# Converting double-precision weights on three engines: the split between VectorE and GpSimd, and two pieces of feed-forward held for the next block

## The chip, the cores and the metric

The kernel runs on one core of a Trainium2 chip. The core has five engines, each with an instruction queue of its own that it works through in order: TensorE (PE, with PEld for its weight loads), VectorE (DVE), ScalarE (ACT), GpSimd (POOL) and SyncE (SP), whose queue here only starts DMAs. Engines wait for each other through semaphores. The metric is the time of one execution in microseconds (us) on the device.

## The reference

Attention in which each query keeps only its 32 largest scores, and then a feed-forward layer with a hardswish gate. The attention's output is the input of the feed-forward layer.

```python
scores = scale * np.matmul(q, k.transpose(0, 1, 3, 2))      # (8, 8, 576, 64) each
kth = np.partition(scores, -32, axis=-1)[..., -32:-31]
scores = np.where(scores >= kth, scores, -1e9)
attn = softmax(scores)                                       # with 1e-9 in the denominator
x = (attn @ v) as (4608, 512)
h = x @ w_in                                                 # (512, 2048)
g = h * np.clip(h + 3.0, 0.0, 6.0) / 6.0
out = g @ w_out                                              # (2048, 512)
```

q, k and v are float32. [...]

## The kernel before

**Duos.** The work is cut into 80 duos. A duo is two pairs of heads and one tile of 128 queries; for the last 64 queries of a batch it is a rest duo, with one tile instead of two for each pair. For each duo TensorE makes the scores (`scores`, L225) into PSUM, and ScalarE copies them to SBUF (L271). VectorE then finds the 32 largest of each row: `top` (L276) takes four rounds of MAX8 (L283), and between them MATCH_REPLACE8 (L287) strikes out what was found. For each of the duo's two halves u (0 and 1) then follow: `shift` on GpSimd (L296, L299), `exp` on ScalarE (L306 and L311, with the sum into `den`, L316), `inverse` on VectorE (the reciprocal, L320), `weights` on GpSimd (L330 scales, L339 splits the words into halves for a transpose), `flip` (a DMA transpose from SP's queue), `join` (L351, which puts the halves together again, on ScalarE or GpSimd), and for both halves together `values` on TensorE (L371) and `place` (L381, a copy to xT on ScalarE).

**Steps.** The order of the work is written out by hand. The main loop takes each duo m through 8 steps i, and in each step VectorE gets one round of `top`. Step i of duo m is slot 8m + i of the whole order. The tables `usual`, `behind`, `early` and `soon` (L570 to L583) say how many steps after a duo's start each of the parts above is put into the queues. For duos 0 and 1 (`early`) the reciprocal comes one step after the exponentials; for the others it comes five steps after them.

**Feed-forward.** Every second duo completes 128 rows of x, and `queue` (L471) then adds a block of 16 pieces: eight of the first matmul (16 matmul records each, L398) and eight of the second (4 records each, L418). After every other one of the first eight, ScalarE reads h (L406, L408), and two pieces later a gate follows on GpSimd (L412, L413). At the end of each step `due` (L639) says how many pieces TensorE gets: one where any are left, a fraction more where 24 or 48 are left, half of it in rest duos. After the last duo the steps go on for three more duos without VectorE work, and then the pieces that are left follow one after another. The outputs of both matmuls, `values` and (in this kernel) the converted `y` share three PSUM buffers (`ps_w`).

**Conversion.** There are 32 chunks of 128 x 512 weights, 16 of w_in and 16 of w_out. `convert` (L96) is a generator, and `convert_step` (L522) advances three chunks by one stage each, once before and once after the first transposes and then once in every step until no chunk is left. A float64 is the words `lo` and `hi`, and they lie side by side, so each is read with a stride of two. For a chunk, in order:

- a DMA into a staging tile `st`;
- on ScalarE `y` = 2 + lo x 2^-51 (L109), into PSUM for the first 24 chunks and straight into the weight's place for the last 8, and the absolute value of `hi` read as a float, into the place of `lo` (L112); on GpSimd a clamp of that (L113);
- two steps later on VectorE a shift left by three bits (L118), and an operation with two inputs that takes the sign bit out of `hi` and puts it into `y` (L119);
- one step later on GpSimd the integer sum of both (L124), which is the float32 weight.

In a step, the sum of one chunk comes first, then VectorE's part of another, then ScalarE's part and the clamp of a third, then the next DMA. In the first four duos `shift` and `exp` stand ahead of the conversion within a step, and `inverse` and `weights` behind it.

**The start.** The first pair is transposed on its own: ScalarE copies its parts out of PSUM one after another (L195 to L197 and L187), and then the first scores in three copies (L271), so that VectorE can begin.

Of the kernel before, what the change touches and what calls it, by code (L numbers as in the profile page):

```python
# [8 lines left out]
AF = mybir.ActivationFunctionType  # L9
ALU = mybir.AluOpType  # L10
F32 = mybir.dt.float32
U32 = mybir.dt.uint32
I32 = mybir.dt.int32
# [11 lines left out]
HI_LEAST = 2.0**-15  # L25
HI_MOST = 122880.0 - 2.0**-7
# [3 lines left out]
def kernel(  # L30
# [9 lines left out]
    nc = tc.nc  # L40
    P = nc.NUM_PARTITIONS
# [3 lines left out]
    JP = J * P  # L45
    R = S - JP
    NHP = H // 2
    NFC = FF // P
    assert 2 * D == P and 2 * R == P and NHP * P == DM and B % 2 == 0
    assert JP == 512 and DM == 512 and TOP_K % 8 == 0  # L50
    scale = 1.0 / float(D) ** 0.5

    def pool(name, bufs, **kw):
        return ctx.enter_context(tc.tile_pool(name=name, bufs=bufs, **kw))
# [8 lines left out]
    gpool = pool("g", 8)  # L63
# [3 lines left out]
    ps_w = pool("ps_w", 3, space=PSUM)  # L67
# [20 lines left out]
    def big():  # L88

        return ps_big.tile([P, 5 * 512], F32, tag="big", name="big")  # L90
# [2 lines left out]

    WC = 512

    def convert(dst, src, early):  # L96

        st = kqpool.tile([P, 2 * WC], U32, tag="kq", name="st")
        nc.sync.dma_start(st[:], src)
        yield
        words = st[:].rearrange("p (n two) -> p n two", two=2)
        lo, hi = words[:, :, 0], words[:, :, 1]
        y = ps_w.tile([P, WC], F32, tag="w", name="y")[:] if early else dst

        nc.scalar.activation(y, lo, AF.Copy, bias=2.0, scale=2.0**-51)  # L109

        a = lo.bitcast(F32)
        nc.scalar.activation(a, hi.bitcast(F32), AF.Abs)  # L112
        nc.gpsimd.tensor_scalar(a, a, HI_MOST, HI_LEAST, ALU.min, ALU.max)  # L113
        yield

        nc.vector.tensor_scalar(lo, lo, 3, None, ALU.logical_shift_left)  # L118
        nc.vector.scalar_tensor_tensor(  # L119
            out=dst.bitcast(U32), in0=hi, scalar=0x80000000, in1=y.bitcast(U32),  # L120
            op0=ALU.bitwise_and, op1=ALU.bitwise_or,
        )
        yield
        nc.gpsimd.tensor_tensor(  # L124
            dst.bitcast(I32), lo.bitcast(I32), dst.bitcast(I32), ALU.add
        )

    def weight_chunks():
# [11 lines left out]
    class Pair:  # L140
# [31 lines left out]

        def transpose(self, first=False):

            kq = kqpool.tile([P, JP + S], F32, tag="kq", name="kq")
            self.kT, self.qT = kq[:, 0:JP], kq[:, JP : JP + S]
            c0 = 2 * JP

            def turn(ps, tiles):
                for i, j in enumerate(tiles):  # L180
                    rows = self.landed[:, j, :, :].rearrange("p h d -> p (h d)")
                    nc.tensor.transpose(ps[:, i * P : (i + 1) * P], rows, ident[:])  # L182

            def copy_left(ps):
                for hh in range(2):
                    d = slice(hh * D, (hh + 1) * D)
                    nc.scalar.copy(self.kr[d, hh, :], ps[d, 0:R])  # L187

            if first:

                ps = [ps_w.tile([P, 512], F32, tag="w", name="kqp") for _ in range(3)]
                turn(ps[0], range(J))
                turn(ps[1], [J, 2 * J])
                turn(ps[2], range(J + 1, 2 * J))
                nc.scalar.copy(self.kT, ps[0][:])  # L195
                nc.scalar.copy(kq[:, JP : JP + P], ps[1][:, 0:P])
                copy_left(ps[1][:, P:])  # L197
                self.later = [
                    (kq[:, JP + P : c0], ps[2][:, 0 : JP - P]),
                    (kq[:, c0 : c0 + R], ps[1][:, P + R : 2 * P]),  # L200
                ]
                return
            ps = big()
            turn(ps, range(2 * J + 1))
            nc.scalar.copy(kq[:, 0:c0], ps[:, 0:c0])
            nc.scalar.copy(kq[:, c0 : c0 + R], ps[:, c0 + R : c0 + 2 * R])
            copy_left(ps[:, c0:])

    class Duo:
# [15 lines left out]
        def scores(self, us=(0, 1)):  # L225

            if us[0] == 0:
                self.sc = scpool.tile([P, 2, 2 * (S + R)], F32, tag="sc", name="sc")
                self.den = mpool.tile([P, 2, 2], F32, tag="den", name="den")
            sc, nu = self.sc[:, us[0] : us[-1] + 1, :], len(us)  # L230
            ps = big()
            heads = [slice(0, D), slice(D, P)]
            qs = slice(self.qt * P, min(self.qt * P + P, S))
            banks = ps[:, 0 : 4 * 512].rearrange("p (n s) -> p n s", s=512)
            left = ps[:, 4 * 512 :]
            if self.rest:


                quarters = [
                    (i, hh, d, heads[u ^ hh])  # L240
                    for i, u in enumerate(us)
                    for hh, d in enumerate(heads)
                ]
                for i, hh, d, to in quarters:
                    pr = self.pairs[us[i]]
                    nc.tensor.matmul(banks[to, i, :], pr.qT[d, qs], pr.kT[d, :])
                for i, hh, d, to in quarters:
                    pr = self.pairs[us[i]]
                    nc.tensor.matmul(banks[to, 2 + i, 0:R], pr.qT[d, qs], pr.kr[d, hh, :])
                nc.gpsimd.memset(sc[:, :, S : S + R], 0.0)  # L250
                nc.scalar.copy(sc[:, :, 0:JP], banks[:, 0:nu, :])
                nc.scalar.copy(sc[:, :, JP:S], banks[:, 2 : 2 + nu, 0:R])
                return
            for i, u in enumerate(us):
                pr = self.pairs[u]
                nc.tensor.matmul(  # L256
                    left[:, i * P : (i + 1) * P], pr.qT[:, qs], pr.kr[:].rearrange("p h r -> p (h r)")
                )
            for i, u in enumerate(us):
                pr = self.pairs[u]  # L260
                for hh, d in enumerate(heads):
                    nc.tensor.matmul(banks[:, 2 * i + hh, :], pr.qT[d, qs], pr.kT[d, :])  # L262
            copies = [
                (sc.rearrange("p u (h s) -> p (u h) s", h=2)[:, :, 0:JP], banks[:, 0 : 2 * nu, :]),
                (sc[:, :, JP : JP + P], left[:, 0 : nu * P].rearrange("p (u r) -> p u r", r=P)),
            ]
            if us == (0,):
                (to, src), rest = copies
                copies = [rest, (to[:, 0, :], src[:, 0, :]), (to[:, 1, :], src[:, 1, :])]
            for copy in copies:  # L270
                nc.scalar.copy(*copy)  # L271

        def row(self, u, t):
            return self.sc[:, u, t * S : (t + 1) * S]
# [171 lines left out]
    ND = len(duos)  # L446
# [4 lines left out]
    left = 0  # L451
# [60 lines left out]
    chunks = list(weight_chunks())  # L512
    landing, converting, adding = [], [], []

    def land(count=1):

        for _ in range(min(count, len(chunks))):
            c = convert(*chunks.pop(0), early=len(chunks) >= NFC // 2)
            next(c)
            landing.append(c)  # L520

# [26 lines left out]
    ps = big()  # L548
    for _ in range(2):
        nc.tensor.matmul(ps[:, 0:DM], w_out[:, 0, 0:P], w_out[:, 0, :])  # L550
    first[0].load(nc.scalar)
    first[1].load()
    land()
    first[2].load()
    land()
    first[0].transpose(first=True)
    duos[0].scores((0,))
    for copy in first[0].later:
# [17 lines left out]
    early = dict(  # L576
        shift0=3, exp0=3, inverse0=4, weights0=4, flip0=5, join0=8,
        shift1=7, exp1=7, inverse1=8, weights1=8, flip1=9, join1=12, values=12, place=13,
    )
# [27 lines left out]
    due = 0.0  # L607
    for m in range(ND + 3):
        u = duos[m] if m < ND else None
        for i in range(8):  # L610
            if u:
                u.top(i // 4, i % 4)
            if m < 4:
                parts(8 * m + i, False)
            convert_step()
            if m == 0 and i in (1, 2):
                first[i + 1].transpose()
            if i == (4 if m == 0 else 1) and m + 1 < ND:
                duos[m + 1].scores()
            if m < 4:  # L620
                parts(8 * m + i, True)
            else:
                parts(8 * m + i)
            if m == 0 and i in (1, 4):
                for p in duos[i // 4].pairs:
                    p.load_values()
            if i == 0:
                p = pair_at(m, 4)
                if p:
                    p.load()  # L630
            if i == 3 and u and u.pairs[0].b and 1 <= m % per_batch <= 2:
                for p in duos[m - 1].pairs:
                    p.load_values()
            if i == 5:
                p = pair_at(m, 5)
                if p:
                    p.transpose()

            due += ((left > 0) + (left >= 24) / 8 + (left >= 48) / 8) / (2 if u and u.rest else 1)  # L639
            piece(int(due))  # L640
            due -= int(due)
    while todo:
# [35 lines left out]
```

## Time and profile before

| | |
|---|---|
| median of 3 runs | 1565.45 us (1564.18 to 1566.11) |
| the profiled execution | 1565.89 us, span 1564.1 us |
| VectorE busy | 1465.7 us (94%) |
| TensorE busy | 1445.2 us (92%) |
| GpSimd busy | 1136.3 us (73%) |
| ScalarE busy | 1098.6 us (70%) |
| L118, L119 (VectorE) | 32 x 896 ns; 24 x 675 ns with `y` in PSUM, 8 x 1041 ns with `y` in SBUF |
| L113, L124 (GpSimd) | 32 x 710 ns; 32 x 1.33 to 1.36 us |
| L109, L112 (ScalarE) | 32 x 630 to 687 ns; 32 x 680 ns |

The span runs from the first to the last instruction of the profile; the execution's time has a little more around it. A group's line gives the line of the kernel, the engine, the operation, the tiles (out<-in), the shapes and the count, then the busy time and the mean duration of one, then the idle time of the engine just before these instructions and what ended it. Busy shares are means over a kernel whose stages differ: the conversion happens in the first 141 us only, and the last 64 us have no VectorE work in them.

### The profile page before, as it was taken

To read this page: it belongs to the slowest core of one execution; us is meant where nothing else is said; L and a number is where in the kernel's file an instruction comes from. 1 tells how busy PE (TensorE), PEld (TensorE's weight loads), DVE (VectorE), ACT (ScalarE), POOL (GpSimd) and SP (SyncE) were. 2 spreads that over 40 slices of the span, in tenths; PEclk is the share of its full clock that TensorE was granted. 3 is DMA by queue.
4 is the path that set the end of the run, shared out by engine and by line. 5 is a ranking of instruction groups with operands and counts; after the bars stand their busy time and mean duration, and the time that the engine had idled before them with its cause. 6 is when DMAs were issued, how large, how long until landed. Compare 5 with 4: busy or idle time off the path is not lost.

```text
span 1564.1 us, 28780 instructions
## 1 busy us (share of the span) xinstructions
PE 1445.2 (92%) x10276; PEld 1033.0 (66%) x10276; DVE 1465.7 (94%) x3106; ACT 1098.6 (70%) x1868; POOL 1136.3 (73%) x1264
## 2 busy tenths in 40 slices
PE   5257798899999999999999999999999999999899
PEld 3143665677767777767776777677777777666675
DVE  6999999999999998999999999999999999999910
ACT  6676777677777777777777777777777777777631
POOL 3769688677777788677777778777777778777761
PEclk7568899999999999999999999999999999999999
DMA  8552445344444445355344454554344555433420
GB/s 225 160 196 57 103 83 113 74 93 81 69 83 99 98 86 108 73 100 93 76 83 85 100 96 83 89 99 98 69 83 83 99 99 92 95 68 68 79 42 14
DMA packets 450319, 144.49 MB, mean 92 GB/s; under 512 B 433280, under 2 KB 441472, under 8 KB 450176
## 3 DMA queue, kind: packets, MB, share of 16 engines
q1 hardware_dynamic: 448976, 142.36, 44.9%
q8 instruction: 81, 1.33, 0.3%
q14 instruction: 62, 0.51, 0.1%
q10 hardware_dynamic: 1200, 0.30, 0.1%
HBM read 45.09 MB, written 9.44 MB: 35 GB/s over the span
## 4 chain that ended last, share of the span: by engine, by line
DVE 42%; PE 42%; POOL 7%; ACT 4%; issue 4%; DMA 2%; SPq 1%; POOLq 0%; DVEq 0%; ACTq 0%
DVE m L283 22%; DVE wk L287 19%; PE h L398 16%; PE acc L418 15%; PE pv L371 5%; PE big L262 3%; POOL e L339 2%; POOL sc L330 1%; POOL g L413 1%; PE big L182 1%; POOL eT L351 1%; DMA t<-e 1%; PE big L256 1%; ACT sc L311 1%; ACT eT L351 1%
## 5 line engine op out<-in xcount | busy, mean ns | idle before, releaser
L283 DVE MAX8 m<-wk 128x8 f32<-128x576 f32 x864 | 614.6, 750 | 2.2
L418 PE MATMUL acc<-w_out,g 128*128 128x512 f32 x1152 | 522.1, 604 | 10.5 <-POOL g L413 10.5
L398 PEld LDWEIGHTS h<-xT,w_in 128*128 128x128 f32 x4096 | 472.1, 193 | 39.4 <-issue 21.7
L398 PE MATMUL h<-xT,w_in 128*128 128x128 f32 x4096 | 485.2, 278 | 14.0 <-ACT xT L381 13.1
L287 DVE MATCH_REPLACE8 wk<-m,wk 128x576 f32<-128x576 f32 x576 | 424.7, 746 | 0.0
L418 PEld LDWEIGHTS acc<-w_out,g 128*128 128x128 f32 x1152 | 214.1, 192 | 256.1 <-issue 234.1
L330 POOL TENSOR_SCALAR sc<-sc,den 128x576 f32<-128x576 f32 x288 | 213.0, 749 | 204.0 <-DVE den L320 177.1
L339 POOL COPY e<-sc 128x2304 uint16<-128x2304 uint16 (+1 forms) x192 | 320.0, 1677 | 10.1
L351 ACT COPY eT<-t 128x2304 uint16<-128x2304 uint16 (+1 forms) x82 | 215.9, 2633 | 57.8 <-DMA t<-e 53.5
L306 ACT ACTIVATE sc<-sc,m 128x576 f32<-128x576 f32 x288 | 210.6, 779 | 57.4 <-DVE m L283 57.0
L311 ACT ACTIVATE sc<-sc,shift 128x576 f32<-128x576 f32 x288 | 220.5, 771 | 40.9 <-POOL shift L299 38.6
L371 PE MATMUL pv<-eT,vm 128*64 128x128 f32 (+1 forms) x2560 | 163.4, 272 | 58.7 <-DVE w_out L119 20.5
L287 DVE MATCH_REPLACE8 wk<-m,sc 128x576 f32<-128x576 f32 x288 | 212.4, 746 | 0.0
L283 DVE MAX8 m<-sc 128x8 f32<-128x576 f32 x288 | 203.8, 746 | 8.9 <-ACT sc L271 8.9
L351 POOL COPY eT<-t 128x2304 uint16<-128x2304 uint16 (+1 forms) x78 | 203.5, 2609 | 7.7 <-DMA t<-e 7.7
L371 PEld LDWEIGHTS pv<-eT,vm 128*64 128x64 f32 x2560 | 134.8, 141 | 110.5 <-issue 23.8
L406 ACT ACTIVATE g<-h,three 128x512 f32<-128x512 f32 x144 | 98.8, 686 | 139.2 <-PE h L398 138.9
L413 POOL TENSOR_TENSOR g<-g,hs 128x512 f32<-128x512 f32 x144 | 184.3, 1280 | 12.2 <-POOL g L412 0.2
L271 ACT COPY sc<-big 128x256 f32<-128x256 f32 (+3 forms) x131 | 136.5, 1094 | 32.2 <-PE big L262 32.1
L412 POOL TENSOR_SCALAR g<-g 128x512 f32<-128x512 f32 x144 | 88.6, 615 | 70.4 <-ACT g L406 60.8
L262 PE MATMUL big<-kq 64*128 64x512 f32 x512 | 131.6, 633 | 0.0
L408 ACT COPY hs<-h 128x512 f32<-128x512 f32 x144 | 83.7, 581 | 0.0
(58 smaller groups left out, 1002.1 us busy)
## 6 DMA issues: line engine op xcount, KB each, us to landing
landed<-in_k_dram SPq DMA_DIRECT2D x64, 128.0 KB, 2.9
st<-in_moe_w_in_dram SPq DMA_DIRECT2D x16, 512.0 KB, 5.3
vm<-in_v_dram SPq DMA_DIRECT2D x64, 128.0 KB, 2.4
st<-in_moe_w_out_dram SPq DMA_DIRECT2D x16, 512.0 KB, 5.3
out_dram<-o SPq DMA_DIRECT2D x32, 256.0 KB, 2.5
landed<-in_q_dram SPq DMA_DIRECT2D x62, 128.0 KB, 2.9
t<-e SPq DMA_TRANSPOSE x160, 4.6
landed<-in_k_dram SPq DMA_DIRECT2D x32, 32.0 KB, 2.6
```

The lines of the kernel that those rows point to most:

```text
L262: nc.tensor.matmul(banks[:, 2 * i + hh, :], pr.qT[d, qs], pr.kT[d, :])
L283: nc.vector.max(self.m[u][:, t, 8 * r : 8 * r + 8], self.cur[t])
L287: nc.vector.match_replace(wk, self.m[u][:, t, 8 * r : 8 * r + 8], self.cur[t], LOWEST)
L306: nc.scalar.activation(row, row, AF.Prelu, bias=m[:, t, TOP_K - 1 : TOP_K], scale=-1.0, alpha=FLAT)
L311: nc.scalar.activation(row, row, AF.Exp, bias=self.less[u][:, t : t + 1], scale=-scale / FLAT, accum_out=self.den[:, u, t : t + 1],)
L330: nc.gpsimd.tensor_scalar(row, row, self.den[:, u, t : t + 1], 1.0, ALU.mult, ALU.mult)
L339: nc.gpsimd.tensor_copy(halves[:, :, to : to + c1 - c0], words)
L351: copy(eT[:, 0 : self.nb, :] .rearrange("p c q -> p (c q)") .bitcast(U16) .rearrange("p (x h) -> p h x", h=2), self.t16[u][:, 0 : 2 * self ...
L371: nc.tensor.matmul(pv[hh * D : (hh + 1) * D, u * w : (u + 1) * w], pr.vm[:, hh, c, :] if c < J else pr.vr[:, hh, :], rhs, start=(c == 0), ...
L398: nc.tensor.matmul(h[:, (f - f0) * P : (f - f0 + 1) * P], w_in[:, i, f * P : (f + 1) * P], xT[:, i, :], start=(i == 0), stop=(i == NHP - 1),)
L413: nc.gpsimd.tensor_tensor(g[:], g[:], hs[:], ALU.mult)
L418: nc.tensor.matmul(acc[:], gs[f // nf][:, f % nf * P : (f % nf + 1) * P], w_out[:, f, :], start=(f == 0), stop=(f == NFC - 1),)
```

## The change

`convert` gets a tile `a` of its own from the pool that also holds the gates' `g` (eight buffers), and uses no PSUM. ScalarE makes the absolute value of `hi` first, and then `y`, which always goes straight to the weight's place. GpSimd clamps `a` and then does a second operation: it compares `hi`, read as a float, with zero and multiplies the outcome by -2^31, which as an integer is the sign bit or zero; this goes into the place of `lo`. On VectorE one operation with two inputs in SBUF shifts `a` and puts the sign bit on it with an exclusive or. GpSimd's sum follows as before.

At the start, three of the first pair's copies out of PSUM (128x128 and twice 64x64) and the first scores' copy of 128x128 go to VectorE.

The rule for pieces, until the last duo, asks for more than two pieces left instead of more than none, so two pieces of a block wait until the next block is queued.

```diff
-    def convert(dst, src, early):
+    def convert(dst, src):
...
-        y = ps_w.tile([P, WC], F32, tag="w", name="y")[:] if early else dst
-
-        nc.scalar.activation(y, lo, AF.Copy, bias=2.0, scale=2.0**-51)
-
-        a = lo.bitcast(F32)
-        nc.scalar.activation(a, hi.bitcast(F32), AF.Abs)
-        nc.gpsimd.tensor_scalar(a, a, HI_MOST, HI_LEAST, ALU.min, ALU.max)
+        a = gpool.tile([P, WC], F32, tag="g", name="a")
+        nc.scalar.activation(a[:], hi.bitcast(F32), AF.Abs)
+        nc.gpsimd.tensor_scalar(a[:], a[:], HI_MOST, HI_LEAST, ALU.min, ALU.max)
+
+        nc.scalar.activation(dst, lo, AF.Copy, bias=2.0, scale=2.0**-51)
+
+        nc.gpsimd.tensor_scalar(
+            lo.bitcast(I32), hi.bitcast(F32), 0.0, -(2.0**31), ALU.is_lt, ALU.mult
+        )
         yield
-        nc.vector.tensor_scalar(lo, lo, 3, None, ALU.logical_shift_left)
+        au = a[:].bitcast(U32)
         nc.vector.scalar_tensor_tensor(
-            out=dst.bitcast(U32), in0=hi, scalar=0x80000000, in1=y.bitcast(U32),
-            op0=ALU.bitwise_and, op1=ALU.bitwise_or,
+            out=au, in0=au, scalar=3, in1=lo,
+            op0=ALU.logical_shift_left, op1=ALU.bitwise_xor,
         )
         yield
         nc.gpsimd.tensor_tensor(
-            dst.bitcast(I32), lo.bitcast(I32), dst.bitcast(I32), ALU.add
+            dst.bitcast(I32), a[:].bitcast(I32), dst.bitcast(I32), ALU.add
         )
...
-            def copy_left(ps):
+            def copy_left(ps, copy=nc.scalar.copy):
                 for hh in range(2):
                     d = slice(hh * D, (hh + 1) * D)
-                    nc.scalar.copy(self.kr[d, hh, :], ps[d, 0:R])
+                    copy(self.kr[d, hh, :], ps[d, 0:R])
...
-                nc.scalar.copy(kq[:, JP : JP + P], ps[1][:, 0:P])
-                copy_left(ps[1][:, P:])
+                nc.vector.tensor_copy(kq[:, JP : JP + P], ps[1][:, 0:P])
+                copy_left(ps[1][:, P:], nc.vector.tensor_copy)
...
             for copy in copies:
-                nc.scalar.copy(*copy)
+                if us == (0,) and copy is rest:
+                    nc.vector.tensor_copy(*copy)
+                else:
+                    nc.scalar.copy(*copy)
...
-            due += ((left > 0) + (left >= 24) / 8 + (left >= 48) / 8) / (2 if u and u.rest else 1)
+            due += ((left > (2 if m < ND - 1 else 0)) + (left >= 24) / 8 + (left >= 48) / 8) / (2 if u and u.rest else 1)
```

More of the change, by code (lines that the diff above doesn't have):

```diff
@@ L517, in land @@
         for _ in range(min(count, len(chunks))):
-            c = convert(*chunks.pop(0), early=len(chunks) >= NFC // 2)
+            c = convert(*chunks.pop(0))
             next(c)
```

## The prediction

> **What bounds the kernel now.** I read the page first: the span, the busy line and the slices.
>
> ```profile
> span 1564.1 us, 28780 instructions
> PE 1445.2 (92%) x10276; PEld 1033.0 (66%) x10276; DVE 1465.7 (94%) x3106; ACT 1098.6 (70%) x1868; POOL 1136.3 (73%) x1264
> ```
>
> VectorE has 98 us without work, nearly all of it before its first MAX8 (at 10.3 us) and after its last (1492.7 us). Between them it has hardly a gap: so a microsecond that VectorE loses or gains anywhere before 1490 us moves the rest of the kernel, and a microsecond of TensorE counts only after that. The conversion lies in the first 141 us, so next I read the busy time of that part in stages of 20 us (columns: engines in the order PE, PEld, DVE, ACT, POOL, each with its instructions; clock; DMA share; GB/s).
>
> ```profile
> 40.00:60.00 20.00, 1.87 (x6) 0.29 (x2) 20.00 (x35) 14.16 (x20) 15.63 (x18) 0.50 0.62 162
> ...
> 120.00:140.00 20.00, 15.91 (x50) 7.75 (x49) 19.17 (x32) 13.32 (x21) 19.33 (x19) 0.83 0.16 31
> ```
>
> VectorE is full in both, but GpSimd, which gets the new instruction, has only 4.4 us in 20 left in the first and nothing in the second. Then the groups by line and shape, for the prices:
>
> ```profile
> L118 DVE TENSOR_SCALAR st<-st 128x512 uint32<-128x512 uint32 x32 | 28.7, 896 | 2.6 <-POOL st L113 2.5
> ...
> L113 POOL TENSOR_SCALAR st<-st 128x512 f32<-128x512 f32 x32 | 22.7, 710 | 46.0 <-ACT st L112 45.4
> ...
> L124 POOL TENSOR_TENSOR w_in<-st,w_in 128x512 int32<-128x512 int32 x16 | 21.2, 1327 | 0.0
> ...
> L119 DVE SCALAR_TENSOR_TENSOR w_in<-st,y 128x512 uint32<-128x512 uint32 x16 | 10.8, 676 | 0.0
> ...
> L119 DVE SCALAR_TENSOR_TENSOR w_out<-st,w_out 128x512 uint32<-128x512 uint32 x8 | 8.3, 1041 | 0.0
> ```
>
> Last I read the instructions in order of time, from one softmax half to the next (start, duration, instruction, idle before it and who ended it): ScalarE's `den`, VectorE's reciprocal of it, and GpSimd between.
>
> ```profile
> 46.40 0.20 ACT L316 ACTIVATE den<-den 128x2 f32<-128x2 f32 x1
> ...
> 62.57 0.20 ACT L316 ACTIVATE den<-den 128x2 f32<-128x2 f32 x1
> ```
> ```profile
> 47.96 0.15 DVE L320 RECIPROCAL den<-den 128x2 f32<-128x2 f32 x1
> ...
> 64.11 0.15 DVE L320 RECIPROCAL den<-den 128x2 f32<-128x2 f32 x1
> ```
> ```profile
> 51.81 0.64 POOL L113 TENSOR_SCALAR st<-st 128x512 f32<-128x512 f32 x1 [1.99 <-ACT st L112]
> 52.55 1.47 POOL L330 TENSOR_SCALAR sc<-sc,den 128x576 f32<-128x576 f32 x2
> 54.08 2.10 POOL L339 COPY e<-sc 128x2304 uint16<-128x2304 uint16 x1
> 56.15 1.46 POOL L124 TENSOR_TENSOR w_in<-st,w_in 128x512 int32<-128x512 int32 x1
> 57.70 0.65 POOL L113 TENSOR_SCALAR st<-st 128x512 f32<-128x512 f32 x1
> 58.31 1.29 POOL L124 TENSOR_TENSOR w_in<-st,w_in 128x512 int32<-128x512 int32 x1
> 59.57 0.84 POOL L113 TENSOR_SCALAR st<-st 128x512 f32<-128x512 f32 x1
> 60.38 0.18 POOL L296 TENSOR_TENSOR shift<-m 128x2 f32<-128x2 f32 x1
> 60.66 0.22 POOL L299 TENSOR_SCALAR shift<-shift 128x2 f32<-128x2 f32 x1
> ```
>
> This is a closed loop in which VectorE has no part. After `den` (46.60) ScalarE does a chunk (1.2 us), the join (2.7) and another chunk (1.3), which releases L113 at 51.81; GpSimd then runs without a gap to the shift (60.88), whose successor on ScalarE, the two exponentials, ends in the next `den` at 62.77. Its period is 16.15 us, the distance of the reciprocals too. VectorE comes to each reciprocal 1.36 us after `den` is there: that is all the room this loop has.
>
> **The change part by part.**
>
> *VectorE's own work.* Out go 32 L118 (28.7 us) and 32 L119 (10.8 + 5.4 + 8.3 = 24.5), together 53.2. In come 32 two-input steps whose inputs both lie in SBUF, for which the eight w_out rows are the nearest: shortest 0.677, mean 1.041, longest 1.78 us. So 21.7 (none waits) to 33.3 us (mean); I take 33.3, since the spread goes with a busy GpSimd (95% there). Alone that is a gain of 20 us, at most 31.5.
>
> *The port.* L118 takes 0.40 us where GpSimd is idle, and up to 1.97 where an instruction of GpSimd is running: it ends 0.3 us after that. L119 with `y` in PSUM always takes 0.67 to 0.68. In the other direction L113 at 59.57 takes 0.84 instead of 0.65 beside an L118, and beside an L119 with both inputs in SBUF L113 takes 1.11 (119.73 us) and L124 1.73 instead of 1.29 (138.28 us). So a new step holds GpSimd up by 0.45 us, where an L118 held it 0.19 and an early L119 nothing. [...]
>
> *GpSimd.* 32 sign instructions are new. The trace has no comparison on GpSimd; the nearest row is L113, also 128x512, one input, two scalar operations, every second word: 0.65 us, 0.60 from start to start. It cannot be below L412's 0.61 by much, and L124 (two inputs, 1.33) is the upper bound. I take 0.60.
>
> *The softmax loop, slots 4 to 16.* Into the stretch from L113 to the shift come three signs (+1.80) and three new steps that hold the port (+1.35, of which 0.37 was there already); the absolute value now ahead of the other half of the chunk on ScalarE releases L113 0.6 us sooner, and L113 on a dense tile saves 0.04 each time. 1.80 + 0.98 - 0.60 - 0.12 = 2.05 us more, period 18.2. Three such loops follow the first reciprocal at 32.30, which itself stays where it is: ScalarE's queue ahead of it waits at 22.69 us for a chunk's DMA, in either kernel. The third loop's reciprocal (80.26) so comes 3 x 2.05 - 1.36 = 4.8 us later. VectorE would need only 9.8 + 4 x 1.09 = 14.2 us per loop (0.60 start to start and 0.49, L118's mean excess, for the port); it waits for `den`, and behind that reciprocal all its MAX8 wait.
>
> *Slots 16 to 31.* Before, GpSimd goes from L330 at 84.84 to the last L113's end at 138.31, with 10.8 us idle (5.18 + 0.23 + 2.98 + 2.44). The start is later by 6.1 (4.8 + 1.36 - 0.6 for the earlier release + 0.6 for the sign ahead of it, rounded down). 13 signs (7.8) and the port (13 x 0.45, less 3.5 that delayed it before: 2.4) add 10.2 us, which eat the idle time; I leave 1.1 us of idle for the 5.18, a wait for ScalarE. That ends at 138.3 + 6.1 + 10.2 - 10.8 + 1.1 = 144.9, and the last conversion step on VectorE, which needs that sign, at 145.6 where the last L119 ended at 141.1: **+4.5 us**, with bounds 0 (all room is found) and +19 (signs at 1.33). Nothing gives it back: VectorE is full from there to 1476 us, but for 4.05 us at 598 and 1.5 later.
>
> *Two pieces kept back.* The feed-forward lags by two pieces from block 0 on. In the middle that costs nothing: TensorE is not what VectorE waits for, and the 13 us in which it waits for xT are covered by VectorE too. At the end:
>
> ```profile
> 1488.00 1.98 PE L371 MATMUL pv<-eT,vm 128*64 128x128 f32 x16 [4.06 <-POOL eT L351]
> ...
> 1546.41 13.90 PE L418 MATMUL acc<-w_out,g 128*128 128x512 f32 x32
> ```
>
> TensorE waits at 1484 us for a join that GpSimd makes, and from 1488 to the end it never pauses. The last duo's steps work one piece each with or without the threshold, so two more pieces stand behind that wait: 2 x 4 matmuls x 0.43 us (13.90 / 32) = 3.4 us. Gates also move two steps back on GpSimd, which may free the shift ahead of VectorE's 2.15 us wait at 1478.8 by some 1.3 us. 2.1 to 3.4, I take **+3.0**; 0 if the wait before 1488 grows shorter by as much.
>
> *The rest.* The first copies moved to VectorE fill its 8.86 us of idle time; the first MAX8 starts up to 0.7 us sooner, but the first conversion step waits for DMA, ScalarE and GpSimd as L118 did at 14.19. `y` leaves PSUM, and TensorE's two waits for it (18.7 and 20.5 us) go; VectorE missed nothing that stood behind them. Both 0, the first bounded by -1. The staging buffers come free one add sooner: DMAs go out a little sooner, 0.
>
> Sum: +4.5 + 3.0 = +7.5 us. The profiled execution took 1565.89 us (span and 1.8 around it), 0.44 above the median shown; 1565.45 + 7.5 = 1573.
>
> **The rivals.**
>
> *Faster: VectorE's work decides.* If GpSimd and ScalarE keep up, the 20 us come out, less 5 chunks x 0.6 before the anchor at 32.3, plus 3.0 at the end: -14, so 1552. For it: VectorE is at 20.00 of 20.00. Against it: the loop. It decides when the loop stays under 16.15 + 1.36 and falls towards 14.2, which the three signs alone (1.8) prevent.
>
> *Even.* The port costs less and ScalarE's earlier release more than I took; the loop grows by its room only, and the idle time of slots 17 to 24 takes the rest. 0 + 3.0: 1568.5.
>
> *The sign is dear.* At L124's 1.33 each sign costs 0.68 more: nine in the loops (6.1), 13 after them (8.8). 1573 + 15 = 1588.
>
> **How the numbers follow.** Forecast 0.62, faster 0.13, even 0.15, dear sign 0.10. A measurement of this kernel tells about 0.2% (3.1 us) from no change, so the limits are 1562.3 and 1568.6: slower 0.62 + 0.10 + 0.04 of the even case, same 0.11, faster 0.13. The range leaves out the faster case and the far end of the dear sign: 1562 to 1584. The forecast's own range is 1568 to 1579.
>
> **What would show it.** Right: VectorE waits 2 to 4 us at reciprocals near 49, 67 and 85 us for `den`, GpSimd 9 of 10 or more from 35 to 150 us, the last conversion step near 145, and TensorE's last stretch without pause about 3 us longer. The signs near 0.65 us. Wrong: no wait at these reciprocals, or the last conversion step before 138 us (VectorE decides); signs above 1 us; or the two pieces at the end filling TensorE's pause.

## The result, and the profile after

The changed kernel takes 1607.11 us (median of 6, 1605.97 to 1609.01), the kernel before on the same chip 1565.78 (1564.18 to 1569.59): a ratio of 1.0263, 95% interval 1.0249 to 1.0277. It is 41 us slower, where the prediction had 7.5 us and a range that ended at 1584.

The direction and the place were as forecast, the size was not. The top of the page of after:

```profile
span 1604.3 us, 28751 instructions
PE 1449.2 (90%) x10276; PEld 1030.6 (64%) x10276; DVE 1459.5 (91%) x3078; ACT 1101.5 (69%) x1864; POOL 1204.5 (75%) x1296
```

VectorE has 6 us less work and a span 40 us longer; GpSimd has 68 us more work. The stages that the prediction read, in after (engines in the order PE, PEld, DVE, ACT, POOL; clock; DMA share; GB/s):

```profile
40.00:60.00 20.00, 3.80 (x9) 1.19 (x8) 12.52 (x24) 7.10 (x12) 18.05 (x16) 0.59 0.47 136
120.00:140.00 20.00, 16.38 (x103) 14.44 (x104) 17.36 (x29) 12.38 (x21) 19.18 (x16) 0.67 0.65 253
```

VectorE, full before, works 12.5 of 20 us in the first stage, and GpSimd is the full one. Two groups of the conversion in after (line, engine, operation, shape, count; busy, mean ns; idle before) say why:

```profile
L112 POOL TENSOR_SCALAR st<-st 128x512 int32<-128x512 f32 x32 | 63.8, 1993 | 2.6
...
L120 DVE SCALAR_TENSOR_TENSOR a<-a,st 128x512 uint32<-128x512 uint32 x32 | 42.4, 1326 | 44.6 <-POOL st L112 44.6
```

L112 is the sign: 1.99 us each, not 0.65. VectorE's waits in after:

```profile
DVE a L120 <- POOL st L112: 44.6, 17, 6.6
DVE den L327 <- ACT den L323: 16.0, 5, 8.0
```

One loop of the softmax in after, GpSimd's instructions in order of time (start, duration, instruction, idle before it):

```profile
57.85 0.61 POOL L108 TENSOR_SCALAR a<-a 128x512 f32<-128x512 f32 x1 [1.30 <-ACT a L107]
58.54 2.00 POOL L112 TENSOR_SCALAR st<-st 128x512 int32<-128x512 f32 x1
60.51 1.27 POOL L125 TENSOR_TENSOR w_in<-a,w_in 128x512 int32<-128x512 int32 x1
61.87 0.94 POOL L108 TENSOR_SCALAR a<-a 128x512 f32<-128x512 f32 x1
62.89 1.99 POOL L112 TENSOR_SCALAR st<-st 128x512 int32<-128x512 f32 x1
64.87 1.89 POOL L337 TENSOR_SCALAR sc<-sc,den 128x576 f32<-128x576 f32 x2
...
75.22 1.97 POOL L112 TENSOR_SCALAR st<-st 128x512 int32<-128x512 f32 x1
77.16 0.20 POOL L303 TENSOR_TENSOR shift<-m 128x2 f32<-128x2 f32 x1
77.44 0.70 POOL L306 TENSOR_SCALAR shift<-shift 128x2 f32<-128x2 f32 x1
```

And VectorE in after, the reciprocal on both sides of such a loop, the last conversion step and the last MAX8:

```profile
57.25 0.17 DVE L327 RECIPROCAL den<-den 128x2 f32<-128x2 f32 x1 [2.02 <-ACT den L323]
...
80.06 0.17 DVE L327 RECIPROCAL den<-den 128x2 f32<-128x2 f32 x1 [2.02 <-ACT den L323]
...
182.04 1.73 DVE L120 SCALAR_TENSOR_TENSOR a<-a,st 128x512 uint32<-128x512 uint32 x1 [3.80 <-POOL st L112]
...
1526.45 1.41 DVE L290 MAX8 m<-wk 128x8 f32<-128x576 f32 x2
```

From L108 at 57.85 to the shift GpSimd has no gap of more than 0.1 us. The period is 22.8 us (16.15 before). The last conversion step ends at 183.8 us where the last L119 ended at 141.1: 42.7 us lost. But the last MAX8 ends at 1527.86 instead of 1492.78: only 35.1 us later, so 7.6 us came back between. And from the last MAX8 to the end it takes 76.4 us instead of 71.3: 5.1 more. 42.7 - 7.6 + 5.1 = 40.2 us, the difference of the spans. Three terms to test: the first is far larger than forecast, the second was not forecast at all, the third is larger. The second and the third are not independent: some 2 us of both are one and the same wait, as the experiments on the held pieces show.

### The profile page after: what moved, and what is told of

The parts are those of the page before. It is cut to its first block, busy times and chain, and to the rows that moved or that the text cites. A ratio compares the mean times of both kernels' runs of the same rounds, so it can differ in the third digit from the quotient of the medians.

```text
span 1604.3 us, 28751 instructions
## 1 busy us (share of the span) xinstructions
PE 1449.2 (90%) x10276; PEld 1030.6 (64%) x10276; DVE 1459.5 (91%) x3078; ACT 1101.5 (69%) x1864; POOL 1204.5 (75%) x1296
## 3 DMA queue, kind: packets, MB, share of 16 engines
q8 instruction: 81, 1.33, 0.3%
## 4 chain that ended last, share of the span: by engine, by line
DVE 79%; POOL 9%; issue 5%; PE 4%; SPq 1%; DMA 1%; ACT 0%; POOLq 0%
DVE m L290 42%; DVE wk L294 37%; POOL st L112 3%; PE acc L425 2%; PE h L405 2%; POOL a L108 1%; POOL w_out L125 1%; POOL sc L337 1%; POOL w_in L125 1%; DMA st<-in_moe_w_in_dram 1%; POOL e L346 1%; DVE den L327 1%; SPq L154 1%; POOL g L420 0%; POOL eT L358 0%
## 5 line engine op out<-in xcount | busy, mean ns | idle before, releaser
L425 PE MATMUL acc<-w_out,g 128*128 128x512 f32 x1152 | 528.6, 608 | 30.1 <-POOL g L420 24.7
L405 PE MATMUL h<-xT,w_in 128*128 128x128 f32 x4096 | 477.7, 277 | 1.7 <-ACT xT L388 1.5
L337 POOL TENSOR_SCALAR sc<-sc,den 128x576 f32<-128x576 f32 x288 | 214.4, 754 | 228.3 <-DVE den L327 226.6
L358 POOL COPY eT<-t 128x2304 uint16<-128x2304 uint16 (+1 forms) x78 | 203.9, 2614 | 14.9 <-DMA t<-e 14.8
L413 ACT ACTIVATE g<-h,three 128x512 f32<-128x512 f32 x144 | 99.1, 688 | 74.4 <-PE h L405 74.1
L278 ACT COPY sc<-big 128x2048 f32<-128x2048 f32 (+3 forms) x130 | 136.2, 1100 | 4.4 <-DVE sc L276 3.4
```

The costliest lines, as they stand in the source:

```text
L337: nc.gpsimd.tensor_scalar(row, row, self.den[:, u, t : t + 1], 1.0, ALU.mult, ALU.mult)
L358: copy(eT[:, 0 : self.nb, :] .rearrange("p c q -> p (c q)") .bitcast(U16) .rearrange("p (x h) -> p h x", h=2), self.t16[u][:, 0 : 2 * self ...
L405: nc.tensor.matmul(h[:, (f - f0) * P : (f - f0 + 1) * P], w_in[:, i, f * P : (f + 1) * P], xT[:, i, :], start=(i == 0), stop=(i == NHP - 1),)
L425: nc.tensor.matmul(acc[:], gs[f // nf][:, f % nf * P : (f % nf + 1) * P], w_out[:, f, :], start=(f == 0), stop=(f == NFC - 1),)
```

## The experiments

**The sign: is it the comparison, the conversion to an integer, or VectorE's step beside it?** Three kernels change only L112 of the changed kernel. sign_clamp makes the same word in another way, with the two operations that L108 also uses: min(hi, 0) and then max with -2^-149, whose word is the sign bit and the lowest bit. Negative weights so differ by at most their lowest bit.

```diff
-            lo.bitcast(I32), hi.bitcast(F32), 0.0, -(2.0**31), ALU.is_lt, ALU.mult
+            lo.bitcast(F32), hi.bitcast(F32), 0.0, -(2.0**-149), ALU.min, ALU.max
```

> The changed kernel with another instruction for the sign: the smaller of hi (read as a float) and zero, and then the larger of that and the smallest negative number, written as a float. It gives the sign bit and at most one unit of the last place more; all else is as changed. Theory 'price of the sign': this form costs about 0.65 us on GpSimd like the clamp L113, the softmax loop's period falls from 22.8 to about 18.2 us, the last conversion step ends near 146 us instead of 183, and the time is near 1568 us. Rival 'the new VectorE step costs it' (two inputs in SBUF, the port held): the sign's price matters little, the last conversion step stays beyond 170 us and the time stays above 1590 us.

1569.33 us against 1565.07: ratio 1.0021 (1.0011 to 1.0031). The groups and the last conversion step of sign_clamp:

```profile
L120 DVE SCALAR_TENSOR_TENSOR a<-a,st 128x512 uint32<-128x512 uint32 x32 | 32.1, 1002 | 24.4 <-POOL st L112 24.4
...
L112 POOL TENSOR_SCALAR st<-st 128x512 f32<-128x512 f32 x32 | 21.3, 665 | 0.0
```
```profile
143.83 1.74 DVE L120 SCALAR_TENSOR_TENSOR a<-a,st 128x512 uint32<-128x512 uint32 x1 [1.03 <-POOL st L112]
```

One instruction written differently takes 38.2 us out of the conversion: its last step ends at 145.57 instead of 183.77. That is the price of 32 comparisons, and with a sign at 0.66 the end lies where the prediction put it, 145.6. The other two kernels split the comparison from the integer output. Each was run once, and both leave the sign out.

```diff
 sign_minmax_int
-            lo.bitcast(I32), hi.bitcast(F32), 0.0, -(2.0**31), ALU.is_lt, ALU.mult
+            lo.bitcast(I32), hi.bitcast(F32), 0.0, -(2.0**31), ALU.min, ALU.max
 sign_cmp_float
-            lo.bitcast(I32), hi.bitcast(F32), 0.0, -(2.0**31), ALU.is_lt, ALU.mult
+            lo.bitcast(F32), hi.bitcast(F32), 0.0, -(2.0**-149), ALU.is_lt, ALU.mult
```

> The changed kernel with a smaller-of and larger-of in the place of the comparison and the multiplication, but still written as an integer (the sign is not computed by it, so that part of the result is left out). If the conversion to an integer on the way out is what makes the sign cost 1.99 us: 2.0 us again, and about 1607 us. If the comparison is: 0.65 us and about 1568 us.

> The changed kernel with the comparison and the multiplication kept, but written as a float (all weights come out negative, the sign is left out). If the comparison is what costs: about 2.0 us and 1607 us. If the conversion to an integer is: 0.65 us and about 1568 us.

sign_minmax_int took 1570.77 us, sign_cmp_float 1605.87. Their sign instructions, the first of sign_minmax_int and the second of sign_cmp_float:

```profile
L112 POOL TENSOR_SCALAR st<-st 128x512 int32<-128x512 f32 x32 | 21.6, 674 | 2.6
```
```profile
L112 POOL TENSOR_SCALAR st<-st 128x512 f32<-128x512 f32 x32 | 64.2, 2006 | 0.0
```

The integer output costs nothing (0.674 us with it, 0.665 with float in sign_clamp), and the comparison with multiplication costs the same with float output (2.01). It is not VectorE's step: with the same steps beside it the sign takes 0.67 as min and max. These kernels do not part the comparison from the multiplication behind it, but another line of the changed kernel does: L337 is a TENSOR_SCALAR of GpSimd with two multiplications.

```profile
L337 POOL TENSOR_SCALAR sc<-sc,den 128x576 f32<-128x576 f32 x288 | 214.4, 754 | 228.3 <-DVE den L327 226.6 <-PE h L405 1.0
```

It takes 0.75 us for 576 columns, 0.67 for 512 in proportion. So these multiplications are not dear, and the comparison is what is left; a comparison without a multiplication was not run.

**The sign off GpSimd.** sign_scalar takes away GpSimd's new instruction as a whole. ScalarE makes a word z in its place (PSUM for 24 chunks, `lo`'s place for 8). For the 24 chunks VectorE's step so has only one input in SBUF, and two things change at once. The sign is left out in this kernel: z is not the sign bit of `hi`.

```diff
+        if early:
+            z = ps_w.tile([P, WC], F32, tag="w", name="z")[:]
+            nc.scalar.activation(z, hi.bitcast(F32), AF.Copy, bias=-0.0, scale=0.0)
...
-        nc.gpsimd.tensor_scalar(
-            lo.bitcast(I32), hi.bitcast(F32), 0.0, -(2.0**31), ALU.is_lt, ALU.mult
-        )
...
-            out=au, in0=au, scalar=3, in1=lo,
+            out=au, in0=au, scalar=3, in1=z.bitcast(U32),
```

> The changed kernel with the sign made by ScalarE: hi, read as a float, times zero plus minus zero, which leaves zero with the sign of hi; into PSUM for the first 24 chunks, into the place of lo for the last 8. Theory 'what GpSimd does and waits for between two softmax halves sets the pace': no sign on GpSimd and no port held in the loops, so 5.3 us on ScalarE to the clamp, 8.4 on GpSimd, 1.9 for the exponentials: period 15.6 us; the last conversion step ends near 136 us instead of 183, and with the held pieces' 2.5 us gain the time is near 1558. Rival 'ScalarE becomes the bound' (32 x 0.65 us more on it): period above 16.2 us and a time of 1563 us or more.

1559.05 us against 1564.58: ratio 0.9963 (0.9949 to 0.9976). The new step on VectorE in sign_scalar, with z in PSUM and in SBUF:

```profile
L123 DVE SCALAR_TENSOR_TENSOR a<-a,z 128x512 uint32<-128x512 uint32 x24 | 16.3, 680 | 10.6 <-POOL a L108 7.6 <-ACT sc L316 3.0
...
L123 DVE SCALAR_TENSOR_TENSOR a<-a,st 128x512 uint32<-128x512 uint32 x8 | 10.9, 1358 | 5.4 <-POOL a L108 4.4 <-POOL g L422 1.0
```

Reciprocals come at 45.00, 60.40 and 75.80: a period of 15.4 us, below the 16.15 of before. So the single step on VectorE is worth something when GpSimd does not pay for it, neither with a sign nor with longer instructions beside that step (L108 takes 0.61 to 0.62 us there from 40 to 70 us, and 0.94 beside an L120 in after); which of the two counts for how much was not separated. The next experiment gives the share of the held pieces (1.8 us of the 5.5), and the rest is the conversion's.

**The two pieces kept back, alone.** hold_alone is the kernel before with the new rule for pieces and nothing else; after_old_rule is the changed kernel with the old rule.

```diff
-            due += ((left > 0) + (left >= 24) / 8 + (left >= 48) / 8) / (2 if u and u.rest else 1)
+            due += ((left > (2 if m < ND - 1 else 0)) + (left >= 24) / 8 + (left >= 48) / 8) / (2 if u and u.rest else 1)
```

> The kernel before with the new rule for pieces alone. Theory 'holding pieces back removes VectorE waits': VectorE's waits for den at 598 (4.05 us), 985 (1.5) and 1479 us (2.15) go, its last MAX8 ends 7.6 us earlier, the stretch after it is 5.1 us longer, so about 2.5 us faster than before: 1563 us. The prediction's reading (nothing in the middle, two pieces more at the end): 3 us slower, 1569 us, with the three waits still there. Rival 'the waits went because the longer conversion shifted everything': the waits stay and the end is 3 to 5 us longer.

> The changed kernel with the old rule for pieces. If the parts add up, the conversion's loss stays and the held pieces' gain of 1.8 us (1563.3 against 1565.1) goes: about 1609 us, with VectorE waits for den near 640 us and at the end again. If the slower conversion had hidden or made the effect of the held pieces: 1607 or less.

hold_alone: 1563.28 us against 1565.07, ratio 0.9987 (0.9977 to 0.9998). after_old_rule: 1607.42 us, ratio 1.0273 (1.0259 to 1.0287). The rule moves neither kernel by more than 0.2% (the changed kernel has 1607.11 us with it). For after_old_rule about 1609 us were expected if the parts add, so this missed by 1.6; its waits came where they were expected, 4.35 us at 641.38 and at the end. The traces show what the sum hides. In hold_alone the last MAX8 ends at 1484.28 (8.5 us sooner than before, of which 0.9 lies ahead of the end of the conversion), and the rest takes 78.1 us instead of 71.3 (6.8 more). In after_old_rule the last MAX8 ends 6.7 us later than in after, and the rest takes 71.2. VectorE's waits in hold_alone, which before were 15.3 us in 5, are

```profile
DVE den L320 <- ACT den L316: 9.7, 2, 8.0
```

so the waits of 4.05, 1.5 and 2.15 us are gone, in after too (16.0 us in 5 there: four of 2.02 in the conversion and one of 7.95 at the end). (The wait of 1.5 us stands at 954.99 us in before, not near 985 as expected.) The largest of them in the trace of before, queue and engines in order of time:

```profile
578.95 2.10 POOL L339 COPY e<-sc 128x2304 uint16<-128x2304 uint16 x1
...
584.79 0.60 ACT L428 ACTIVATE o<-acc 128x512 f32<-128x512 f32 x1 [3.25 <-PE acc L418]
...
585.42 0.36 SPq L430 DMA_DIRECT2D out_dram<-o  x1
...
585.88 17.25 SPq L345 DMA_TRANSPOSE t<-e  x4
...
592.26 2.79 ACT L351 COPY eT<-t 128x2304 uint16<-128x2304 uint16 x1 [3.69 <-DMA t<-e]
...
597.90 0.20 ACT L316 ACTIVATE den<-den 128x1 f32<-128x1 f32 x1
598.14 0.16 DVE L320 RECIPROCAL den<-den 128x1 f32<-128x1 f32 x1 [4.05 <-ACT den L316]
```

The words for a flip are ready at 581.05, but no flip is issued until 585.88: SP's queue goes in order, and ahead of it stands the DMA of a block's output, which waits for `o` from ScalarE, which waits for TensorE's `acc`. ScalarE's join then waits 3.69 us for the late transpose, and the exponentials and `den` behind it are late for VectorE. In hold_alone the feed-forward lags by two pieces, and the output's DMA stands elsewhere among the flips:

```profile
574.56 8.26 SPq L345 DMA_TRANSPOSE t<-e  x2
588.84 0.36 SPq L430 DMA_DIRECT2D out_dram<-o  x1
```

The flips are issued by 582.82, and none of VectorE's reciprocals there waits. The wait of 1.5 us in before has the same order of events: words ready at 940.49, the output's DMA at 943.03, the flip at 943.49, then a join that waits 2.90 us. In hold_alone the flip in this place goes out at 942.35, as its words are ready (942.32). Where the old rule stands, one or two such waits are there (4.05 and 1.46 in before, 5.12 in copies_alone below, 4.35 in after_old_rule); where pieces are held, none is.

The wait of 2.15 us is another matter: it moved. In before, a gate (L412 and L413 on GpSimd) stands in the queue ahead of the shift whose `den` VectorE then waits for, with only L330 and L339 between; after the last MAX8 VectorE waits 5.90 us for the last reciprocal:

```profile
1470.85 0.61 POOL L412 TENSOR_SCALAR g<-g 128x512 f32<-128x512 f32 x1
...
1476.39 0.20 POOL L296 TENSOR_TENSOR shift<-m 128x2 f32<-128x2 f32 x1
...
1478.82 0.17 DVE L320 RECIPROCAL den<-den 128x2 f32<-128x2 f32 x1 [2.15 <-ACT den L316]
...
1498.68 0.17 DVE L320 RECIPROCAL den<-den 128x2 f32<-128x2 f32 x1 [5.90 <-ACT den L316]
```

In after, where gates come two pieces later, no gate stands there, but one stands ahead of the last join and the last shift:

```profile
1528.79 0.61 POOL L419 TENSOR_SCALAR g<-g 128x512 f32<-128x512 f32 x1
...
1530.69 2.76 POOL L358 COPY eT<-t 128x2304 uint16<-128x2304 uint16 x1
...
1533.38 0.20 POOL L303 TENSOR_TENSOR shift<-m 128x2 f32<-128x2 f32 x1
...
1535.81 0.17 DVE L327 RECIPROCAL den<-den 128x2 f32<-128x2 f32 x1 [7.95 <-ACT den L323]
```

VectorE's last wait is 2.05 us longer for it. So of the 7.6 us that after gains ahead of the last MAX8, 5.5 are gained (4.05 and 1.46), and the other 2.15 only change their place.

At the end, TensorE in after:

```profile
1523.09 1.98 PE L378 MATMUL pv<-eT,vm 128*64 128x128 f32 x16 [3.15 <-POOL eT L358]
...
1533.50 1.09 PE L378 MATMUL pv<-eT,vm 128*64 128x128 f32 x16 [1.34 <-POOL eT L358]
...
1534.75 7.13 PE L425 MATMUL acc<-w_out,g 128*128 128x512 f32 x16
```

and in hold_alone:

```profile
1489.94 1.09 PE L371 MATMUL pv<-eT,vm 128*64 128x128 f32 x16 [2.52 <-POOL eT L351]
...
1491.18 8.83 PE L418 MATMUL acc<-w_out,g 128*128 128x512 f32 x16
```

Before, there were 8 matmuls in this place (3.70 us, from 1498.02, 5.24 us after the last MAX8) and no wait since 1488. In after there are 16 (7.13 us, 3.4 more), and they start 6.89 us after the last MAX8, 1.65 later; most of that is the second wait, 1.34, for the join at 1530.69 that now stands behind the gate. 3.4 + 1.65 = 5.1. In hold_alone the same two terms are 5.1 and 1.66; the 16 matmuls take 8.83 us there at a granted clock of 0.81, where in after it is 1.00.

**Keeping the gain and not the end.** hold_catch is the kernel before with the pieces held back until four duos before the end only, and a sixteenth of a piece more per step in those four duos, so that the two pieces are caught up while VectorE still works.

```diff
-            due += ((left > 0) + (left >= 24) / 8 + (left >= 48) / 8) / (2 if u and u.rest else 1)
+            due += ((left > (2 if m < ND - 4 else 0)) + (left >= 24) / 8 + (left >= 48) / 8 + (ND - 4 <= m < ND) / 16) / (2 if u and u.rest else 1)
```

> The kernel before with two pieces held back up to the fourth-last duo, and then 1/16 piece more for each step, so that from slot 631 on the queues stand as in the kernel before. If the held pieces' gain in the middle (waits at 598 and near 985 us, 5.5 us) and their cost at the end (two pieces behind the last wait, 5.1 us) are separate things: the middle's gain stays and the cost goes, near 1559.6 us (1557.5 if the wait at 1479 us stays away too). If the end is longer for another reason: 1563 as with the rule alone.

1559.36 us against 1564.58: ratio 0.9972 (0.9960 to 0.9984). TensorE after the last join in hold_catch:

```profile
1489.93 1.09 PE L371 MATMUL pv<-eT,vm 128*64 128x128 f32 x16 [0.55 <-POOL eT L351]
...
1491.18 3.70 PE L418 MATMUL acc<-w_out,g 128*128 128x512 f32 x8
```

Eight matmuls as before. The last MAX8 ends at 1486.34, 6.4 us sooner than before, and the rest takes 71.0 us. Of VectorE's waits the one of 2.15 us is back, and the last is the short one again (5.91):

```profile
1472.38 0.17 DVE L320 RECIPROCAL den<-den 128x2 f32<-128x2 f32 x1 [2.13 <-ACT den L316]
```

So the 5.5 us of the two waits behind SP's queue stay gained, the moved gate is back in its place, and the end costs nothing.

**The first copies, alone.** copies_alone is the kernel before with the change's edits of `copy_left`, of the first pair's copies and of the first scores' copy.

> The kernel before with the first copies on VectorE alone. Prediction's step: VectorE's first MAX8 up to 0.7 us sooner, and nothing of it left at the reciprocal of 32.3 us, which waits for a chunk's DMA: no change (within 1 us). Rival: the first operations' 0.7 us carry through: 1564.4 us.

1564.69 us against 1564.58: ratio 0.9998 (0.9989 to 1.0007). The reciprocal that the prediction called fixed comes at 32.11 (32.30 before). Nothing gained or lost, as forecast. The time alone could not tell 0.7 us from nothing; the reciprocal, 0.19 us sooner, shows that the 0.7 is not carried through.

**Both gains together.** scalar_catch is the changed kernel with the sign on ScalarE, this time a true sign, and hold_catch's rule.

```diff
+            nc.scalar.activation(z, hi.bitcast(F32), AF.Prelu, scale=2.0**-20, alpha=2.0**80)
```

> The changed kernel with the sign bit made by ScalarE instead of GpSimd (one ACTIVATE of hi as a float, multiplied by 2^-20 where positive and by 2^60 where negative, written as int32: 0, or the lowest int32, which is the sign bit; into PSUM for the first 24 chunks and into the place of lo for the last 8), and with the rule of hold_catch for the pieces. Theory (GpSimd's sign is the whole loss of the conversion; the held pieces gain in the middle and the catch-up gives the end back): the loop stays at sign_scalar's 15.4 us, and the time is sign_scalar's 1559.05 less the 3.9 that hold_catch gained over hold_alone: 1555. Rival (VectorE's waits that the held pieces removed and the gain of the conversion are the same microseconds, so they do not add): 1558 to 1560, no better than hold_catch's 1559.4.

1554.23 us (1553.38 to 1555.37) against 1566.08: ratio 0.9927 (0.9911 to 0.9944), the fastest kernel of the case. The page of scalar_catch, and its groups of the sign:

```profile
span 1553.6 us, 28726 instructions
PE 1442.6 (93%) x10276; PEld 1027.8 (66%) x10276; DVE 1443.7 (93%) x3078; ACT 1119.1 (72%) x1896; POOL 1131.2 (73%) x1264
```
```profile
L112 ACT ACTIVATE z<-st 128x512 int32<-128x512 f32 x24 | 14.9, 622 | 0.0
...
L116 ACT ACTIVATE st<-st 128x512 int32<-128x512 f32 x8 | 5.5, 684 | 0.3
```

VectorE has 22 us less work than before, GpSimd 73 us less than in after, and ScalarE has the 20.4 us of the sign (14.9 + 5.5) and is 72% busy. The last MAX8 ends at 1482.30, 4.0 sooner than in hold_catch; the rest takes 71.3 us. The expected sum (1555) held, so the gain of the conversion and that of the held pieces are not the same microseconds.

## Why the prediction was right and wrong

- **The step that failed is the sign's price:** "It cannot be below L412's 0.61 by much, and L124 (two inputs, 1.33) is the upper bound. I take 0.60." It takes 1.99 us, outside both bounds. The bound was chosen by the number of inputs and the shape, and no row showed a comparison: L124 bounds a two-input sum, not another operation. The measured price put through the prediction's own working: from clamp to add it is 2.66 us in after (57.85 to 60.51) and 1.18 in sign_clamp (59.91 to 61.09), so 1.48 more for each sign. Three in a loop make 4.4, and 18.2 + 4.4 = 22.6 where 22.8 was measured. The prediction's 22 signs (9 in the loops, 13 behind them) make 32.6, so +4.5 becomes +37.1, where +42.7 was measured. 2.15 of the difference is the first reciprocal, which the prediction said stays at 32.30: it comes at 34.45, because the shift ahead of it now stands behind signs of 2 us on GpSimd (in sign_clamp it comes at 32.07). Some 3.4 us were not traced further.
- The dear-sign rival had the right mechanism and gave it 0.10. At 1.33 it came to 1588; its price was bounded by the same wrong row. The runs show 1.99 us for the comparison and 0.67 for min and max of the same shape, a factor of three.
- **The loop and the slots behind it** come out right in sum once the price is right: in sign_clamp, the last conversion step ends at 145.57 (145.6 forecast). Inside they differ: the period is 17.56 us (48.81, 66.37, 83.93), not 18.2, and VectorE waits for the sign (24.4 us in 10) where it was to wait for `den`. So that the total agrees to 0.1 us is partly luck: its parts do not agree as well.
- **The port** was priced at 0.45 us for each new step. No run shows a port; what the traces show is that instructions of GpSimd take longer beside the step, by 0.33 to 0.48 us: in after, L108 at 61.87 takes 0.94 beside an L120 (0.61 alone), and the two L337 1.89 (1.47 before). The shift's L306 takes 0.70 instead of 0.22, beside the L120 that the sign before it has just released. With z in PSUM the new step takes 0.67 to 0.69 us in sign_scalar, each of the 24 times.
- **VectorE's own work** was priced at 1.041 each; it is 1.33 in after and 1.00 in sign_clamp. It costs nothing there, since VectorE waits anyway.
- **"In the middle that costs nothing"** failed in its sign. It gains 5.5 us, by two waits of VectorE that the prediction had seen and named (4.05 and 1.5) without asking what made them. The answer, in SP's queue, was in the trace of before.
- **At the end, "+3.0"** came out near its size. The 3.4 us of the extra matmuls were right. The prediction then took off 0.4 for gates that move away from the shift ahead of the 2.15 us wait. That wait goes as a whole, but the gate then stands ahead of the last join and gives 1.65 us back, which the prediction did not see: 3.4 - 2.15 + 1.65 = 2.9. So the 0.4 was near 0.5 by luck. Middle and end together make -2.5 us where +3.0 was forecast, and hold_alone's -1.8 us agrees.
- First copies and `y` out of PSUM at nothing: copies_alone shows it for the copies; `y` was not tried by itself.
- **The faster rival** did not need a dear sign to fail: with the sign at 0.66 (sign_clamp) the loop's period is still 17.56 us, above the 17.51 up to which the rival had it decide. With the sign off GpSimd (sign_scalar against hold_alone, both with held pieces) the last MAX8 ends 5.1 us sooner. That is less than the 17 us which the rival gave the conversion: the period falls to 15.4 us, not to 14.2, and VectorE still waits ahead of its new step for the clamp (7.6 + 4.4 us) and for ScalarE (3.0).

## What to carry to other kernels

Price an instruction by a row with the same operation, not by one with the same shape: where the trace has no such row, the upper bound must leave room for another kind of operation, and the range must reach that far. If a condition can be written as min and max, try that before a comparison on GpSimd (0.67 us against 1.99 here); where GpSimd is full and ScalarE is not, the same bit came cheaper from ScalarE (a loop of 15.4 us in scalar_catch, 45.65 to 61.05, and of 17.56 in sign_clamp). And ask of each wait of the bounding engine, before calling the middle of a kernel full, which queue made it: here a rule for another engine's work moved the stores in SP's queue and took two waits, 5.5 us, away. A wait that is gone from one place is a gain only if it does not stand in another: the third one, 2.15 us, had moved behind the last MAX8.

## What the runs showed of the hardware

- A GpSimd TENSOR_SCALAR of 128x512 with is_lt and mult takes 1.99 us with int32 output (after) and 2.01 with float (sign_cmp_float); with min and max it takes 0.674 with int32 output (sign_minmax_int) and 0.665 with float (sign_clamp). With two multiplications, 128x576 takes 0.75 (after).
- In after, a VectorE step with two SBUF inputs that starts within 0.1 us after the start of a GpSimd add (1.25 to 1.29 us) takes 1.73 to 1.76 us, where the one at 77.37 takes 0.67 (60.57: it ends 0.55 us after the add).
- On ScalarE, Prelu with scale 2^-20 and alpha 2^80, written as int32, serves as the sign word in scalar_catch, and the weights get their signs by it: 0.62 us for 128x512 into PSUM, 0.68 into SBUF.
- On TensorE, in hold_alone, eight `acc` matmuls behind a pause of 3.17 us take 5.40 us at a granted clock of 0.68, and sixteen behind one of 2.52 take 8.83 at 0.81; in after, sixteen behind one of 1.34 take 7.13 at 1.00. Whether the pause sets the clock was not tested.
